# A static scheduler's hand-over estimate goes from 250 to 350, and the first attention's tasks get positions from -32 on

## The chip, the core and the metric

The kernel runs on one core of a Trainium2 chip. TensorE (PE in the profile) multiplies, VectorE (DVE) and ScalarE (ACT) do the elementwise work, GpSimd (POOL) builds the masks once, and SyncE (SP) issues every DMA. The metric is the device time in microseconds (us) of one execution of the whole program; lower is better.

## What is computed

An attention over 4 batches of 8 heads, 576 positions, 64 numbers per head, feeds a network of two layers, all in float32 accuracy:

```python
scores = scale * np.matmul(q, k.transpose(0, 1, 3, 2))
mask_local = (rel >= 0) & (rel < stride)                       # heads 0 to 3, stride 32
mask_strided = (rel >= 0) & (pos % stride == pos.T % stride)   # heads 4 to 7
attn = softmax(np.where(masks, scores, -1e9));  x = attn @ v   # 2304 rows of 512
h = np.maximum(np.maximum(x @ w1, x @ w2), x @ w3)             # 512 -> 768
x = h @ w_out                                                  # 768 -> 512
h = x @ w_in;  g = np.maximum(h, 0) + alpha * np.minimum(h, 0) # 512 -> 2048
out = g @ w_out2                                               # 2048 -> 512
```

## The kernel before

**Arithmetic.** Each float32 operand of the two layers is kept as a pair, a rounded high part and the remainder, and each product is made of three matmuls (high with high, high with low, low with high). The weights arrive as 64-bit numbers. `from_double` turns a block of them into float32 words: a DMA into one of three staging buffers (`raw`), one ScalarE pass (L427, the rebasing) and two VectorE passes (L431 and L433, the word). `split_tasks` then makes the pair: a ScalarE cast (L237) and a VectorE subtraction (L240). Weights of the first layer stay on the chip (18 gate blocks, named by block f and gate g, and 6 output blocks). Weights of the second layer are combined in pairs (`sums`, L500), split, and stored to HBM through two staging tiles (`wst`) for later.

**Attention.** A unit is (batch, head pair cc, half hf). Pairs 2 and 3 are strided heads, 0 and 1 local ones. A unit is a list of tasks: scores on TensorE (L304), per tile a masking that also finds the row minimum (VectorE, L312) and an exponential (ScalarE, L319), a reciprocal (VectorE, L330 and L331), a multiplication by it for each head (`normalise`, on VectorE at L252 or ScalarE at L250), transposes on TensorE (L345), a copy out of PSUM (`keep`, L237, on either engine), the products with v (`values`, L370), and the split of the result into the pair x (a ScalarE cast at L237, a VectorE subtraction at L240).

**First layer.** A gate unit is 12 matmuls (L530) followed by a copy (L616) or a maximum (L619); after the third gate the result is split into h (L625, L240). An output unit is 18 matmuls (L552) and a copy (L599).

**Who sets the order.** Everything up to about 328 us (attention of all four batches, first layer of batches 0 to 2, all weights) is recorded as tasks of a `Weave`. Each task has an engine or two to choose from with an estimated cost in ns, a position `pos`, the things it needs, and the buffers it makes. `Weave.run` plays through the tasks with these estimates and emits them one by one. The engine on which a task could start earliest is served; of its tasks that could start within 120 ns of the first, the one with the lowest position is taken. A task's result counts as there `DELAY` ns after its end. What comes out is a fixed order on every engine; on the chip each engine follows its own order and waits by semaphores. Gate and output units of batch b have positions from 44 b on. Attention units of the first batch have positions spread from `first` to `last` (L719 and L720):

```python
first, last = (-40, -8) if b == 0 else ((b - 1) * NUNITS + (16 if b == 1 else 3), b * NUNITS - 3)
step = (last - first) / (len(ATT_UNITS) + 2)
```

After the weave come the first layer of the last batch and the second layer, written out in a fixed order that this change does not touch. Rings bound what may run ahead: 8 PSUM banks, 2 q and k tiles, 2 v tiles, 3 score tiles, 3 `raw`, 8 words, 2 `wst`.

Of the kernel before, what the change touches and what calls it, by code (L numbers as in the profile page):

```python
# [2 lines left out]

# [35 lines left out]
NUNITS = 2 * (3 * NF1 + NCC)  # L39
# [4 lines left out]
class Weave:  # L44
# [6 lines left out]

    DELAY = {"PE": 300, "ACT": 250, "DVE": 250, "SP": 2300}

    URGENT = 1000

    def __init__(self, rings):
# [4 lines left out]
    def add(self, engines, emit, pos, needs=(), gives=(), makes=(), uses=(), mode=None, slack=0):  # L63
        t = len(self.tasks)
        if engines[0][0] != "PE" and any(key in self.banks for key in uses):
            pos -= self.URGENT
        self.banks.update(key for ring, key in makes if ring == "bank")
        self.tasks.append((engines, emit, pos, needs, makes, mode, slack))
        for ring, key in makes:
            if ring in self.order:  # L70
                self.order[ring].append(key)
        for e in gives:
            self.givers.setdefault(e, []).append(t)
        for key in [key for _, key in makes] + list(uses):
            self.users.setdefault(key, []).append(t)
# [16 lines left out]
                    at = max(at, done[u])  # L92
        return at

    def run(self):
        free = dict.fromkeys(self.DELAY, 0)
        left = [sum(len(self.givers[e]) for e in task[3]) for task in self.tasks]
        takers = {}
        for t, task in enumerate(self.tasks):
            for e in task[3]:  # L100
                for g in self.givers[e]:
                    takers.setdefault(g, []).append(t)
        at = [0] * len(self.tasks)
        ready = {t for t, n in enumerate(left) if not n}
        done, mode = {}, None
        while ready:
            options = {}
            for t in ready:
                engines, _, pos, _, makes, m, slack = self.tasks[t]
                when = self.place(makes, done)  # L110
                if when is None:
                    continue
                when = max(when, at[t] + slack)
                best = None
                for e, cost in engines:
                    start = max(when, free[e])
                    if best is None or start + cost < best[0] + best[2]:
                        best = (start, e, cost)
                start, e, cost = best
                if m is not None:  # L120
                    start += 100 * (m != mode)
                options.setdefault(e, []).append((start, pos - (m is not None and m == mode), t, cost))
            pick = None
            for e, c in options.items():
                first = min(o[0] for o in c)
                o = min((o for o in c if o[0] <= first + 120), key=lambda o: (o[1], o[0], o[2]))
                if pick is None or o[0] < pick[1][0]:
                    pick = (e, o)
            e, (start, _, t, cost) = pick
            _, emit, _, _, makes, m, _ = self.tasks[t]  # L130
            ready.remove(t)
            emit(e)
            for ring, key in makes:
                self.made[ring].append(key)
            mode = mode if m is None else m
            free[e] = start + cost
            done[t] = start + cost + self.DELAY[e]
            for u in takers.get(t, ()):
                left[u] -= 1
                same = e == "PE" == self.tasks[u][0][0][0]  # L140
                at[u] = max(at[u], start + cost if same else done[t])
                if not left[u]:
                    ready.add(u)
        assert len(done) == len(self.tasks)


@with_exitstack
def attention_maxout_prelu_kernel(
# [85 lines left out]
    add, tl = weave.add, {}  # L234
# [34 lines left out]
    def load_task(b, cc, pos):  # L269
        qk, vk = ("q", b, cc), ("v", b, cc)  # L270

        def emit_qk(_):
            q = qkp.tile([P, S], F32, tag="q", name="q")
            nc.sync.dma_start(q, qT[b, cc])
            k = qkp.tile([P, S + 32 * (cc < 2)], F32, tag="k", name="k")
            nc.sync.dma_start(k, kTl[b, cc] if cc < 2 else kTs[b, cc - 2])
            tl[qk] = q, k

        def emit_v(_):
            v = tl[vk] = vp.tile([P, 6 if cc < 2 else 5, 2, D], F32, tag="v", name="v")  # L280
            nc.sync.dma_start(v, vl[b, cc] if cc < 2 else vs[b, cc - 2])

        add(load(592), emit_qk, pos, gives=[qk], makes=[("q", qk)])
        add(load(350), emit_v, pos + 1, gives=[vk], makes=[("v", vk)])

    def attention_tasks(b, cc, hf, pos, step):

        u = (b, cc, hf)
        nq, nk, tiles = geometry(cc, hf)
        n = len(tiles)  # L290
        slack = 1500 if b else 0
        ek, qk, vk = ("e", u), ("q", b, cc), ("v", b, cc)
        banks = [("sc", u, j) for j in range(2)]

        def scores(_):
# [12 lines left out]
            makes=[("bank", key) for key in banks] + [("e", ek)], uses=[qk], mode="scores")  # L308
# [25 lines left out]
        for j in range(2):  # L334
# [13 lines left out]
            def keep(e, trk=trk, ptk=ptk):  # L348
# [3 lines left out]
                gives=[("nrm", u, j)], uses=[ek])  # L352
            add((("PE", 95 * n),), transposes, pos + step, needs=[("nrm", u, j)], gives=[trk],
                makes=[("bank", trk), ("pt", ptk)], uses=[ek], mode="transposes", slack=slack)
# [3 lines left out]
        pvk = ("pv", u)  # L358
        halves = [hf] if cc < 2 else [0, 1]
        xks = [("x", b, cc, h) for h in halves]  # L360
        fresh = [k for k in xks if k not in weave.users]

        def values(_):
# [6 lines left out]
                    nc.tensor.matmul(pv[D * j:D * (j + 1), nq * i:nq * (i + 1)], v[:nk, t, j, :],  # L370
                                     tl["pt", u, j][:nk, nq * i:nq * (i + 1)], start=True, stop=True)

        add((("PE", 2 * n * 85),), values, pos + 2 * step, needs=[vk] + [("pt", u, j) for j in range(2)],
            gives=[pvk], makes=[("bank", pvk)] + [("x", k) for k in fresh],
            uses=[vk] + [("pt", u, j) for j in range(2)] + xks, mode="values", slack=slack)

        def parts(h):
# [8 lines left out]
        for h in halves:  # L386
# [3 lines left out]
                needs=[pvk], gives=[hik], uses=[pvk])  # L390
# [325 lines left out]
    build_constants()  # L716
    nc.sync.dma_start(alpha_sb, alpha)
    for b in range(B):
        first, last = (-40, -8) if b == 0 else ((b - 1) * NUNITS + (16 if b == 1 else 3), b * NUNITS - 3)  # L719
        step = (last - first) / (len(ATT_UNITS) + 2)  # L720
        for i, (cc, hf) in enumerate(ATT_UNITS):
            if i in (0, 2, 4, 5):
                load_task(b, cc, first + step * i - 8)
            attention_tasks(b, cc, hf, first + step * i, step)
# [351 lines left out]
```

## Time and profile before

| | us |
|---|---|
| median of 3 runs (770.6 to 776.38) | 774.55 |
| the profiled execution | 772.29 |
| its span, first to last instruction | 770.2 |
| TensorE matmul busy | 744.1 (97%) |
| TensorE weight loads busy | 723.2 (94%) |
| VectorE busy | 594.6 (77%) |
| ScalarE busy | 457.9 (59%) |

A share is an average over the whole span. How the engines stand in a single stretch is in the rows further down.

### The profile page before, as it was taken

The numbers are of one execution on the slowest core, as the hardware profiler recorded it, in microseconds if no ns is written. First come the engines' busy times: TensorE is split into PE (matmuls) and PEld (weight loads), VectorE is DVE, ScalarE is ACT, GpSimd is POOL, SyncE is SP. The second block draws the span as 40 slices with busy tenths as digits, with TensorE's granted clock in tenths as the row PEclk, the third lists the DMA queues.
The fourth block names the chain that finished last, engine by engine and source line by source line (L and its number), as shares of the span: only waits on it lengthen the run. The fifth ranks groups of instructions, "written<-read, shape, count | busy, mean of one in ns | idle before, by whom it ended". The sixth has DMA issues, their size and how long they took to land.

```text
span 770.2 us, 16100 instructions
## 1 busy us (share of the span) xinstructions
PE 744.1 (97%) x5704; PEld 723.2 (94%) x5704; DVE 594.6 (77%) x1658; ACT 457.9 (59%) x1238; POOL 3.2 (0%) x16
## 2 busy tenths in 40 slices
PE   5899999999989999999999999999999999999997
PEld 4689898999989999999999999999999999999997
DVE  5899998779777796326457988878888877888884
ACT  6997796656768487304246566634656644556561
POOL 1000000000000000000000000000000000000000
PEclk9899999999999999999999999999999999999999
DMA  7467768876879865365947789999888999877361
GB/s 243 157 233 250 222 233 289 297 247 247 291 262 310 274 205 170 120 243 209 342 157 249 264 290 304 381 393 364 286 286 311 347 403 327 271 250 255 119 204 53
DMA packets 85471, 199.37 MB, mean 259 GB/s; under 512 B 10640, under 2 KB 40848, under 8 KB 85392
## 3 DMA queue, kind: packets, MB, share of 16 engines
q1 hardware_dynamic: 85392, 198.35, 74.7%
q8 instruction: 45, 0.74, 0.4%
q14 instruction: 34, 0.28, 0.1%
HBM read 148.51 MB, written 49.81 MB: 258 GB/s over the span
## 4 chain that ended last, share of the span: by engine, by line
PE 60%; DVE 17%; DMA 10%; ACT 8%; issue 3%; SPq 1%; DVEq 0%; ACTq 0%
PE ph L947 20%; PE po L790 15%; PE bank L530 14%; PE bank L552 7%; DMA wh<-w 4%; ACT e L319 2%; DVE word L433 2%; DVE g L784 2%; DMA raw<-in_w 2%; DVE c L794 2%; DVE w L240 2%; PE bank L304 1%; DVE word L431 1%; DVE t L619 1%; PE bank L370 1%
## 5 line engine op out<-in xcount | busy, mean ns | idle before, releaser
L530 PE MATMUL bank<-x,w 128*128 128x288 f32 x1728 | 236.8, 297 | 4.5 <-DVE x L240 1.4
L530 PEld LDWEIGHTS bank<-x,w 128*128 128x128 f32 x1728 | 231.3, 189 | 6.7 <-ACT pt L237 1.7
L947 PE MATMUL ph<-x,w 128*128 128x384 f32 x1008 | 203.3, 337 | 1.1 <-DVE c L952 1.1
L790 PE MATMUL po<-w,g 128*128 128x256 f32 x1296 | 183.8, 282 | 1.7 <-DVE g L784 0.6
L790 PEld LDWEIGHTS po<-w,g 128*128 128x128 f32 x1296 | 175.5, 189 | 4.2 <-DVE g L784 3.2
L947 PEld LDWEIGHTS ph<-x,w 128*128 128x128 f32 x1008 | 168.3, 188 | 2.1 <-DVE c L952 1.8
L952 DVE TENSOR_TENSOR c<-ph,c 128x384 f32<-128x384 f32 x168 | 90.8, 553 | 33.1 <-PE ph L947 32.2
L783 ACT CAST g<-c 128x384 fp32r<-128x384 f32 x96 | 48.5, 505 | 89.7 <-DVE c L934 56.5
L552 PE MATMUL bank<-h,w 128*128 128x288 f32 x576 | 79.5, 297 | 0.4 <-DVE t L619 0.4
L552 PEld LDWEIGHTS bank<-h,w 128*128 128x128 f32 x576 | 76.8, 188 | 1.5 <-DVE t L619 0.6
L240 DVE TENSOR_TENSOR w<-word,w 128x512 fp32r<-128x512 f32 x88 | 55.4, 635 | 26.8 <-ACT w L237 26.5
L319 ACT ACTIVATE e<-e,nm 96x128 f32<-96x128 f32 (+2 forms) x176 | 67.9, 392 | 8.1 <-DVE nm L312 8.0
L904 ACT ACTIVATE c<-c 128x384 f32<-128x384 f32 x96 | 50.4, 525 | 34.0 <-DVE c L952 33.0
L237 ACT CAST w<-word 128x512 fp32r<-128x512 f32 x88 | 50.8, 582 | 31.8 <-DMA wh<-w 15.9
L905 ACT ACTIVATE c<-c,nalpha 128x384 f32<-128x384 f32 x96 | 59.2, 617 | 3.1
L908 DVE SCALAR_TENSOR_TENSOR c<-c 128x384 f32<-128x384 f32 x96 | 52.9, 551 | 8.9 <-ACT c L905 8.9
L784 DVE TENSOR_TENSOR g<-c,g 128x384 fp32r<-128x384 f32 x96 | 52.7, 549 | 1.9 <-ACT g L783 1.9
L784 DVE TENSOR_TENSOR g<-k,g 128x384 fp32r<-128x384 f32 x72 | 36.7, 548 | 14.4 <-ACT g L783 14.4
L427 ACT ACTIVATE word<-raw 128x512 f32<-128x512 f32 x56 | 37.2, 676 | 9.6 <-DMA raw<-in_w 4.8
L433 DVE SCALAR_TENSOR_TENSOR word<-raw,word 128x512 uint32<-128x512 uint32 x56 | 38.8, 692 | 1.9
L619 DVE TENSOR_TENSOR t<-bank,t 128x288 f32<-128x288 f32 x72 | 32.3, 449 | 7.6 <-PE bank L530 4.1
L783 ACT CAST g<-k 128x384 fp32r<-128x384 f32 x72 | 33.4, 516 | 7.8 <-PE po L790 4.4
(72 smaller groups left out, 683.3 us busy)
## 6 DMA issues: line engine op xcount, KB each, us to landing
w<-wh SPq DMA_DIRECT2D x72, 512.0 KB, 4.9
raw<-in_w SPq DMA_DIRECT2D x50, 512.0 KB, 4.6
w<-wo SPq DMA_DIRECT2D x48, 512.0 KB, 5.8
w<-wp SPq DMA_DIRECT2D x36, 512.0 KB, 6.0
wh<-w SPq DMA_DIRECT2D x24, 512.0 KB, 3.5
xd<-xst SPq DMA_DIRECT2D x28, 384.0 KB, 3.3
x<-xd SPq DMA_DIRECT2D x28, 384.0 KB, 8.1
wp<-w SPq DMA_DIRECT2D x24, 256.0 KB, 3.2
```

The lines of the kernel that those rows point to most:

```text
L240: nc.vector.tensor_tensor(out=out_, in0=x, in1=y, op=ALU.subtract)
L319: nc.scalar.activation(tl[ek][:nq, j, i, :nk], tl[ek][:nq, j, i, :nk], AF.Exp, bias=tl["nm", u][:nq, j, i:i + 1], scale=-1.0, accum_out=tl ...
L433: nc.vector.scalar_tensor_tensor(out=a, in0=raw[:, :, 0], scalar=29, in1=a, op0=ALU.logical_shift_right, op1=ALU.bitwise_or)
L530: nc.tensor.matmul(acc, words["gate", f, g][:, wi, cc * P:(cc + 1) * P], xt[b, cc, hf][:, xi, :], start=n == 0, stop=n == 3 * NCC - 1)
L552: nc.tensor.matmul(acc, words["mix", f][:, wi, dc * P:(dc + 1) * P], st["h", hf, f][:, xi, :], start=n == 0, stop=n == 3 * NF1 - 1)
L783: nc.scalar.copy(g[:, 0], x)
L784: return g, lambda: nc.vector.tensor_tensor(out=g[:, 1], in0=x, in1=g[:, 0].bitcast(F32), op=ALU.subtract)
L790: nc.tensor.matmul(bank[:, NH * half:NH * (half + 1)], g[:, gi, t * P:(t + 1) * P], w[:, wi, off:off + NH], start=first and i == 0, stop=l ...
L905: nc.scalar.activation(a, a, AF.Copy, scale=nalpha[:, f:f + 1])
L908: nc.vector.scalar_tensor_tensor(out=a, in0=h, scalar=0.0, in1=a, op0=ALU.max, op1=ALU.add)
L947: nc.tensor.matmul(bank, words["h", n, i][:, wi, off + c * P:off + (c + 1) * P], x2h[blk, k, c][:, xi, :], start=m == 0, stop=m == 5)
L952: nc.vector.tensor_tensor(out=out_, in0=bank, in1=other, op=ALU.add)
```

## The change

Two numbers of the plan change. A task that ends on ScalarE or VectorE now counts as handed over 350 ns after its end, not 250. The first batch's attention units get positions from -32 to -8, not from -40 to -8, so that the step between two units is 2.4 and not 3.2. `run` is divided into `plan`, which makes the order, and the loop that emits it. The other settings of `plan` have the values that stood there before (120, 100, 1.0, no random shift). For strided units, the second half's `values` now needs the first half's to have been placed (`begun`), as the first half makes the x tile that both fill.

```diff
-    DELAY = {"PE": 300, "ACT": 250, "DVE": 250, "SP": 2300}
-
     URGENT = 1000
@@
-    def run(self):
-        free = dict.fromkeys(self.DELAY, 0)
+    def plan(self, seed=None, near=120, change=100, slack=1.0, delay=350, shift=0.0):
+
+        rng = random.Random(seed)
+        sway = [rng.uniform(-shift, shift) if task[2] > -self.URGENT / 2 else 0.0 for task in self.tasks]
+        delays = {"PE": 300, "ACT": delay, "DVE": delay, "SP": 2300}
+        self.made = {ring: [] for ring in self.rings}
+        free = dict.fromkeys(delays, 0)
@@
-                when = max(when, at[t] + slack)
+                when = max(when, at[t] + slack * wait)
@@
-                o = min((o for o in c if o[0] <= first + 120), key=lambda o: (o[1], o[0], o[2]))
+                o = min((o for o in c if o[0] <= first + near), key=lambda o: (o[1], o[0], o[2]))
@@
-            done[t] = start + cost + self.DELAY[e]
+            done[t] = start + cost + delays[e]
@@
+    def run(self, **settings):
...
+        for t, e in self.plan(**settings):
+            self.tasks[t][1](e)
@@
-        add((("PE", 2 * n * 85),), values, pos + 2 * step, needs=[vk] + [("pt", u, j) for j in range(2)],
-            gives=[pvk], makes=[("bank", pvk)] + [("x", k) for k in fresh],
+        begun = ("x begun", b, cc)
+        add((("PE", 2 * n * 85),), values, pos + 2 * step,
+            needs=[vk] + [("pt", u, j) for j in range(2)] + ([begun] if cc >= 2 and hf else []),
+            gives=[pvk] + ([begun] if cc >= 2 and not hf else []), makes=[("bank", pvk)] + [("x", k) for k in fresh],
@@
-        first, last = (-40, -8) if b == 0 else ((b - 1) * NUNITS + (16 if b == 1 else 3), b * NUNITS - 3)
+        first, last = (-32, -8) if b == 0 else ((b - 1) * NUNITS + (16 if b == 1 else 3), b * NUNITS - 3)
```

The change moves instructions on all engines throughout the weave. In the changed kernel a line number of the weave's tasks is 10 to 12 higher (L240 is L250, L431 is L443). Three places follow.

VectorE in the first batch's attention, before: the first gate weight's word (L431, L433) stands between the reciprocal of the last strided unit and its multiplication.

```order
L252 TENSOR_SCALAR e<-e,rc 108x108 x3
L330 TENSOR_SCALAR rc<-sm 126x2x2
L331 RECIPROCAL rc<-rc 126x2x2
L431 TENSOR_SCALAR word<-word 128x512
L433 SCALAR_TENSOR_TENSOR word<-raw,word 128x512
L252 TENSOR_SCALAR e<-e,rc 126x126 x2
```

VectorE, changed: the same word (now L443, L445) stands 33 rows further down, behind the masking of two more local units.

```order
L322 ISA e,nm<-bank,mask_l 96x128
L322 ISA nm 96x1
L262 TENSOR_SCALAR e<-e,rc 96x128 x3
L340 TENSOR_SCALAR rc<-sm 96x6
L341 RECIPROCAL rc<-rc 96x6
L443 TENSOR_SCALAR word<-word 128x512
L445 SCALAR_TENSOR_TENSOR word<-raw,word 128x512
L262 TENSOR_SCALAR e<-e,rc 96x128 x6
```

The word moved behind attention work; in the old place the multiplications of the strided unit (x4) follow the reciprocal at once.

TensorE where the first layer of batch 2 begins (216 us in the trace), before: a gate unit of batch 2 (L530 x12) stands ahead of batch 1's output units (L552).

```order
L304 MATMUL bank<-k,q 108x108 x6
L370 MATMUL bank<-pt,v 64x96 x12
L345 MATMUL bank<-ident,e 128x96 x12
L530 MATMUL bank<-x,w 128x288 x12
L370 MATMUL bank<-pt,v 64x96 x12
L552 MATMUL bank<-h,w 128x288 x54
L530 MATMUL bank<-x,w 128x288 x24
```

The same place, changed.

```order
L314 MATMUL bank<-k,q 108x108 x6
L380 MATMUL bank<-pt,v 64x96 x12
L355 MATMUL bank<-ident,e 128x96 x12
L564 MATMUL bank<-h,w 128x288 x18
L380 MATMUL bank<-pt,v 64x96 x12
L564 MATMUL bank<-h,w 128x288 x54
L542 MATMUL bank<-x,w 128x288 x96
```

All four output units now come before the first gate unit of batch 2.

ScalarE at the same place, before: two casts of second-layer weights and two rebasings stand ahead of the casts of x and the four copies of transposes.

```order
L616 COPY t<-bank 128x288
L237 CAST w<-word 128x512 x2
L427 ACTIVATE word<-raw 128x512 x2
L625 CAST h<-t 128x288
L237 CAST x<-bank 128x288 x2
L237 COPY pt<-bank 128x288 x4
```

The same place, changed.

```order
L247 CAST w<-word 128x256
L637 CAST h<-t 128x288
L247 CAST x<-bank 128x288
L329 ACTIVATE e,sm<-e,nm 108x108 x2
L247 CAST x<-bank 128x288
L247 COPY pt<-bank 128x288 x3
L247 CAST w<-word 128x512 x2
```

The two casts moved behind x and the copies, of which the fourth went to VectorE.

## Rows read from the trace of the kernel before

**Rows 1.** Busy time by stretch: window, its length, busy us of each engine, clock, DMA.

```profile
0.00:44.20 44.20, 31.73 (x278) 24.95 (x278) 31.56 (x195) 35.95 (x149) 3.22 (x16) 0.92 0.61 201
44.20:125.20 81.00, 78.36 (x654) 74.58 (x655) 76.75 (x232) 66.19 (x199) 0.00 (x0) 1.00 0.74 246
125.20:225.20 100.00, 96.48 (x810) 92.88 (x812) 80.65 (x285) 66.11 (x218) 0.00 (x0) 0.98 0.78 268
...
328.00:770.20 442.20, 434.68 (x3081) 430.75 (x3080) 336.17 (x712) 224.90 (x467) 0.00 (x0) 1.00 0.78 274
```

**Rows 2.** TensorE in order of time: start, us, what, and the idle time before.

```profile
27.27 0.72 PE L345 MATMUL bank<-ident,e 96*128 96x96 f32 x3 [1.59 <-DVE e L252]
...
35.59 1.84 PE L530 MATMUL bank<-x,w 128*128 128x288 f32 x12
...
43.14 0.53 PE L530 MATMUL bank<-x,w 128*128 128x288 f32 x2
44.48 15.78 PE L530 MATMUL bank<-x,w 128*128 128x288 f32 x117 [0.81 <-DVE w L240]
```

**Rows 3.** Busy time from VectorE's first instruction to the third weight's remainder.

```profile
6.79:44.43 37.64, 30.20 (x266) 23.39 (x264) 31.79 (x196) 34.90 (x149) 0.00 (x0) 0.91 0.60 202
```

**Rows 4.** VectorE in order of time.

```profile
20.25 0.39 DVE L431 TENSOR_SCALAR word<-word 128x512 uint32<-128x512 uint32 x1
20.67 0.69 DVE L433 SCALAR_TENSOR_TENSOR word<-raw,word 128x512 uint32<-128x512 uint32 x1
...
27.85 0.68 DVE L252 TENSOR_SCALAR e<-e,rc 96x128 f32<-96x128 f32 x3
28.44 0.45 DVE L237 COPY pt<-bank 128x288 f32<-128x288 f32 x1
...
37.32 0.17 DVE L330 TENSOR_SCALAR rc<-sm 96x6 f32<-96x6 f32 x1 [1.02 <-ACT e L319]
...
42.61 0.26 DVE L312 CUSTOM_DVE_ANT_0 e<-bank,mask_s 108x108 f32<-108x108 f32 x1
...
43.74 0.69 DVE L240 TENSOR_TENSOR w<-word,w 128x512 fp32r<-128x512 f32 x1
...
57.76 0.69 DVE L240 TENSOR_TENSOR w<-word,w 128x512 fp32r<-128x512 f32 x1
```

**Rows 5.** ScalarE in order of time.

```profile
34.47 0.99 ACT L250 ACTIVATE e<-e,rc 96x128 f32<-96x128 f32 x3
35.36 0.38 ACT L237 COPY pt<-bank 128x288 f32<-128x288 f32 x1
35.63 0.41 ACT L319 ACTIVATE e<-e,nm 96x128 f32<-96x128 f32 x1
...
37.19 0.61 ACT L237 CAST w<-word 128x512 fp32r<-128x512 f32 x1
...
38.84 1.24 ACT L427 ACTIVATE word<-raw 128x512 f32<-128x512 f32 x2
```

**Rows 6.** Busy time and granted clock (the column after POOL) around the two slow-clock stretches.

```profile
24.00:28.00 4.00, 1.98 (x15) 1.11 (x11) 3.70 (x23) 4.00 (x21) 0.00 (x0) 0.87 0.74 250
28.00:32.00 4.00, 4.00 (x32) 3.27 (x34) 3.86 (x23) 3.68 (x16) 0.00 (x0) 0.50 0.36 106
...
222.00:225.00 3.00, 2.95 (x12) 2.90 (x12) 2.97 (x14) 3.00 (x13) 0.00 (x0) 0.51 0.98 298
```

**Rows 7.** TensorE's later waits in the weave, in order of time.

```profile
125.20 1.88 PE L530 MATMUL bank<-x,w 128*128 128x288 f32 x12 [1.36 <-DVE x L240]
...
220.50 0.47 PE L345 MATMUL bank<-ident,e 96*128 96x96 f32 x3 [1.45 <-DVE t L619]
222.05 3.13 PE L530 MATMUL bank<-x,w 128*128 128x288 f32 x12 [1.08 <-ACT pt L237]
```

**Rows 8.** VectorE at a second-layer weight, in order of time.

```profile
213.65 0.69 DVE L240 TENSOR_TENSOR w<-word,w 128x512 fp32r<-128x512 f32 x1 [2.41 <-ACT w L237]
```

**Rows 9.** The chain of waits, in order of time: start, us, what.

```profile
57.91 4.64 DMA raw<-in_w
```

More of the change, by code (lines that the diff above doesn't have):

```diff
@@ L1 @@
 import math
+import random
 from contextlib import ExitStack
@@ L93, in place @@
         return at
-    def run(self):
-        free = dict.fromkeys(self.DELAY, 0)
-        left = [sum(len(self.givers[e]) for e in task[3]) for task in self.tasks]
[L98 to L102, printed above, removed]
+    def plan(self, seed=None, near=120, change=100, slack=1.0, delay=350, shift=0.0):
[4 more added lines that the diff above has]
+        free = dict.fromkeys(delays, 0)
+        left = [sum(len(self.givers[e]) for e in task[3]) for task in self.tasks]
         at = [0] * len(self.tasks)
         ready = {t for t, n in enumerate(left) if not n}
-        done, mode = {}, None
+        done, mode, order = {}, None, []
         while ready:
@@ L108, in run @@
             for t in ready:
-                engines, _, pos, _, makes, m, slack = self.tasks[t]
+                engines, _, pos, _, makes, m, wait = self.tasks[t]
                 when = self.place(makes, done)
@@ L120, in run @@
                 if m is not None:
-                    start += 100 * (m != mode)
-                options.setdefault(e, []).append((start, pos - (m is not None and m == mode), t, cost))
+                    start += change * (m != mode)
+                options.setdefault(e, []).append(
+                    (start, pos + sway[t] - (m is not None and m == mode), t, cost))
             pick = None
@@ L129, in run @@
             e, (start, _, t, cost) = pick
-            _, emit, _, _, makes, m, _ = self.tasks[t]
+            makes, m = self.tasks[t][4:6]
             ready.remove(t)
-            emit(e)
+            order.append((t, e))
             for ring, key in makes:
@@ L136, in run @@
             free[e] = start + cost
-            done[t] = start + cost + self.DELAY[e]
-            for u in takers.get(t, ()):
+            done[t] = start + cost + delays[e]
+            for u in self.takers.get(t, ()):
                 left[u] -= 1
@@ L144, in run @@
         assert len(done) == len(self.tasks)
+        return order
+    def run(self, **settings):
+        self.takers = {}
+        for t, task in enumerate(self.tasks):
+            for e in task[3]:
+                for g in self.givers[e]:
+                    self.takers.setdefault(g, []).append(t)
+        for t, e in self.plan(**settings):
+            self.tasks[t][1](e)
 @with_exitstack
```

## The prediction

> **What bounds the kernel now.** I read the busy time by stretch first. From 44.2 us on TensorE works almost without a gap: 78.4 of 81.0 us, then 96.5 of 100 us, and 434.7 of 442.2 us in the part that the change leaves alone. Only the first 44.2 us are different: TensorE 31.7, VectorE 31.6, ScalarE 36.0 [rows 1]. The work of TensorE is the same before and after, so a new order is worth what TensorE waits less, or runs less at a low clock, before 328 us. The rows give the stock. Idle TensorE time is 12.5 us up to 44.2, 2.6 up to 125.2, 3.5 up to 225.2 [rows 1]. To this comes the clock: 0.50 of 28 to 32 us and 0.51 of 222 to 225 us, that is its 1.2 GHz level [rows 6]. Twelve gate matmuls took 3.13 us there and 1.88 us at 125.2, so the second low stretch cost 1.25 us [rows 7].
>
> The order of time shows who is late. In the first attention TensorE waits for multiplications by VectorE (1.59 us) and at 44.48 for the remainder of the third gate weight (0.81 us); two of that unit's twelve matmuls ran at 43.14, so in effect the unit began at 44.2 [rows 2]. Later waits are the x of batch 1 (1.36 us at 125.20), a maximum (1.45 us) and copies of transposes (1.08 us) at 220 to 222 [rows 7].
>
> **The count itself.** The trace shows a hand-over directly: VectorE's remainder ends at 43.74 + 0.69 = 44.43 and TensorE's matmul starts at 44.48 [rows 2, 4]. That is 0.05 us; both 250 and 350 ns are longer. The change therefore doesn't make the plan truer to one hand-over; it only puts other work between maker and user. What follows goes by the order alone. The split into plan and emission, and the settings that keep their values, move nothing. The added need orders two `values` groups of equal work and adds no instruction; it costs nothing, since the other group stands ready on TensorE.
>
> **First stretch, up to the third weight.** TensorE has the same tasks ahead of the first product on the third gate weight in both orders, so only the time of that weight counts. Ahead of it on VectorE, five copies (0.45 each), one multiplication (0.59, from 27.85 to 28.44) and a maximum (0.45) leave, 3.3 us; three multiplications (one of them two thirds as long, 1.6) and three copies (1.35) come, 2.9 us [rows 4]. On ScalarE, three multiplications (0.89, 0.89, 0.6), three copies (0.27), a rebasing (0.6) and two exponential steps (1.56 from 35.63 to 37.19) leave, 5.3 us; one multiplication and five copies come, 2.2 us [rows 5]. In that time VectorE is idle for 37.64 - 31.79 = 5.85 us and ScalarE for 2.7 us [rows 3]. ScalarE, the fuller one, loses 3.1 us of work; the gain is at most VectorE's idle time, 5.85 us and the 0.4.
>
> How much of that is got I worked out by following the tasks. Up to 17 us both orders go at the pace of TensorE's unchanged first tasks. The first gate weight's word, made from 20.25 to 21.36 before [rows 4], now comes after the maskings of two more units, so its remainder arrives last of all that the first product needs. That costs two steps more on VectorE ahead of the product (0.59 and 0.69); against it, ScalarE reaches the x of the second local unit 0.8 us of work earlier and VectorE 0.3 us. I take the first product at the old time, 35.6 [rows 2], between 34.7 (0.9 us earlier, if TensorE keeps its clock in the scores and values ahead of it) and 36.9 (both added steps in full).
>
> From there VectorE's queue is known, and no wait shows in it: a copy 0.45, a reciprocal 0.51 (37.32 to 37.83 in the row's own place), a word 1.1 (0.42 from 20.25 to 20.67, and 0.69), a multiplication 0.59, the third weight's word 1.1, the second weight's remainder 0.69, x 0.45, five pairs of maskings at 0.38 (three take 1.13 from 42.61 to 43.74), the third remainder 0.69. The sum is 7.5 us, against 8.84 now (35.59 to 44.43), of which 1.02 is a wait for an exponential [rows 2, 4]. So the third weight is there at 43.1, not 44.43, and TensorE starts on it 1.1 us sooner than the 44.2. **A = -1.1 us**, bounds -5.9 and +0.2 (the product at 36.9).
>
> **Up to 125 us.** VectorE is the pace here: busy 76.75 of 81.0 us [rows 1], and it hands over the x for which TensorE waits 1.36 us [rows 7]. Ahead of that x, three remainders of second-layer weights (0.69 each at most) and four subtractions of `sums` (0.45 each, an estimate from the copy of a like width) leave VectorE, two pairs of maskings come (0.8), and seven multiplications and five copies take the place of four and six (+1.3 by the durations above). One of those remainders is of half width. That makes about 1.3 us less in all. On TensorE the scores of one unit of batch 2 (0.8 us) now stand ahead of the same product. TensorE comes 1.1 us earlier with 0.8 us more to do, VectorE 1.1 + 1.3 us earlier: the wait closes. **B = -1.4 us**, bounds -2.6 (all idle time of this stretch) and +1.2 (A given back, if VectorE only keeps its old time).
>
> **At 216 to 225 us.** The output units now cover the wait for x: 18 matmuls stand between the transposes and the values, 54 behind. Two casts and two rebasings are out of ScalarE's way. But VectorE stood idle for 2.41 us just before, for a cast that waited for a store's buffer [rows 8], and the maximum that frees TensorE's bank is behind such a remainder in both orders. If the stores keep their time, VectorE has from 213.65 on, in the new order, a remainder 0.69, an h 0.45, a half remainder 0.45, a maximum 0.45, four subtractions 1.8, a maximum 0.45, three pairs of maskings 1.13 and the last h 0.45. That is 5.9 us of durations that overlap by some 0.1 us each, so it ends near 219. TensorE, now 2.5 us ahead, waits there about as long as it does now and may fall to 1.2 GHz again. It then starts at 219 where it started at 222.05: 3.05 us earlier, so C adds 0.55. If the stores move up with everything else, both waits (2.53) and the 1.25 of clock go: 3.8. I take **C = -0.7**, near the lower end, because the row shows a wait for a store and not for TensorE; bounds -3.8 and +2.6 (all that was won is waited for here).
>
> **Sum.** 1.1 + 1.4 + 0.7 = 3.2 us. The profiled execution becomes 772.29 - 3.2 = 769.1. It lies 2.3 us under the median of the runs shown; on that scale 774.55 - 3.2 = **771.4 us**, 0.4% faster. One per cent (7.7 us) is about what a measurement of this kernel can tell from no change, so this counts as no change.
>
> **Rivals.** *The gain is waited away.* The stores of the second layer's weights begin some 6 us of VectorE work later in the new order, and the stretch up to 225 us ends when they do. Then TensorE is ahead at 125 us and back at its old time at 225 us: 774.5 us. For it speaks the 2.41 us; against it, that the casts at the place itself stand no later in ScalarE's order.
>
> *The clock.* Before each low stretch TensorE was busy for half of the time or less: 1.98 of 4.0 us from 24 to 28 [rows 6], and 2.53 us idle in two waits at 220 to 222 [rows 7]. If the new order closes those gaps, TensorE stays at 2.4 GHz: A is 0.9 us better, C is the full 3.8, and the sum is 2.0 + 1.4 + 3.8 = 7.2 us: 767.4 us. Against it: the multiplication that starts the second transposes of the first local unit comes only 0.6 us earlier by the count above, so 1 of the 1.59 us gap stays. The Trainium skill, "TensorE: Matmul & The Clock Gate", section "What's actually happening", says that the throttled state is the default and activity releases it; by that rule a first attention with fewer gaps would be spared the low stretch as well. The trace's two low stretches, each behind idle time, agree.
>
> *Slower: the weights come late.* The first weight's word moves from 21 to about 28 us, as it now stands behind the multiplication that starts TensorE's transposes at 27.27 [rows 2]; the second's moves back too. There are three staging buffers, so the fourth and fifth fetches start that much later. A fetch takes 4.64 us to land [rows 9]. The place is 45 to 70 us; the ninth weight's remainder ends at 58.45 [rows 4] and TensorE takes it up at 44.2 + 9 x 1.6 = 58.6, a margin of 0.15 us. By my count the margin becomes 1 us, as the third word comes earlier. It decides from the point where the fourth word is more than 1 us behind it: TensorE then waits one landing for each of two weights, 9.3 us, less the 1.1 won and the 3.9 of later waits that this fills (1.36, 1.45 and 1.08): +4.3, 778.9 us.
>
> *Not doing what it says* would be an order that hardly changes; it is excluded, as the order of all engines differs.
>
> **How the numbers follow.** Forecast (1 to 6 us faster) 0.55; gain waited away 0.2; clock 0.13; slower 0.12. The range takes the first two whole, half of the clock's and some of the slower one's: 767.0 to 777.0. Faster by over 1% (under 766.8) needs the clock's case and a little more: 0.08. Slower by over 1% (above 782.3) needs late weights twice over: 0.04. The rest is 0.88.
>
> **What would show it.** Right: the first gate matmuls start at 34.7 to 36.9 us, the long run of them by 43 us, the wait for x near 122 us is gone, and the part behind the weave lasts 442 us as before. Wrong: a wait of gate matmuls for VectorE's remainders (w) between 45 and 70 us; a wait for a copy behind a cast that waits for a store near 135 us; new low-clock stretches. I would be wrong by more than the range if VectorE stood idle in the first 44 us for longer than now.

## The result and the profile after

The changed kernel takes 765.94 us (median of 6 runs, 764.72 to 767.51) beside 774.51 us for the kernel before on the same chip: a ratio of 0.990, 95% interval 0.988 to 0.993. Twice more beside other runs it came to 0.993 (0.990 to 0.995) and 0.991 (0.989 to 0.993). Over 98 runs on the later chips the kernel before had medians of 772.0 to 773.2 us, so the gain is 6.4 to 8.6 us. 3.2 were forecast, and the time lies 1.1 us under the range.

The profiled execution took 764.85 us (span 762.9). TensorE in order of time, after (start, us, what, idle time before):

```profile
14.16 1.10 PE L355 MATMUL bank<-ident,e 126*126 126x126 f32 x4
...
26.47 0.72 PE L355 MATMUL bank<-ident,e 96*128 96x96 f32 x3 [2.22 <-DVE e L262]
...
35.53 3.23 PE L542 MATMUL bank<-x,w 128*128 128x288 f32 x12
...
42.35 17.86 PE L542 MATMUL bank<-x,w 128*128 128x288 f32 x133
...
117.89 0.82 PE L314 MATMUL bank<-k,q 64*108 64x108 f32 x12
...
121.48 1.00 PE L314 MATMUL bank<-k,q 64*126 64x126 f32 x8 [0.49 <-ACT pt L247]
...
211.08 0.82 PE L314 MATMUL bank<-k,q 64*108 64x108 f32 x12
...
214.62 2.64 PE L564 MATMUL bank<-h,w 128*128 128x288 f32 x18 [0.44 <-DVE nm L322]
...
318.20 19.20 PE L542 MATMUL bank<-x,w 128*128 128x288 f32 x144
```

These answer to [rows 2, 7]. The first gate product starts where it was forecast (35.53; 35.59 before), but its twelve matmuls take 3.23 us and not 1.84. The wait for x of batch 1, the two waits at 220 to 222 us and the slow product there are gone; 0.49 us of waiting for a copy and 0.44 for VectorE are left at these places. Busy time and granted clock (the column after POOL) around those places, after; they answer to [rows 6]:

```profile
24.00:28.00 4.00, 1.78 (x14) 1.44 (x14) 3.93 (x24) 4.00 (x21) 0.00 (x0) 0.78 0.74 246
28.00:32.00 4.00, 4.00 (x37) 3.27 (x34) 3.44 (x23) 3.05 (x11) 0.00 (x0) 0.50 0.71 223
32.00:36.00 4.00, 3.21 (x26) 2.50 (x23) 3.34 (x20) 3.43 (x15) 0.00 (x0) 0.50 0.14 56
36.00:40.00 4.00, 4.00 (x26) 3.50 (x26) 3.51 (x11) 3.04 (x12) 0.00 (x0) 0.51 0.39 108
...
44.00:60.00 16.00, 16.00 (x123) 16.00 (x122) 15.51 (x34) 13.43 (x41) 0.00 (x0) 1.00 0.81 253
...
216.00:225.00 9.00, 9.00 (x84) 8.72 (x83) 6.81 (x18) 7.29 (x24) 0.00 (x0) 1.00 0.70 229
```

The clock fell at the end of the 2.22 us wait and stayed at its 1.2 GHz level until almost 40 us, twice as long as before. At 216 to 225 us it is 1.00. From 44 to 60 us TensorE is busy for all 16 us, and the run of gate matmuls there takes 0.134 us for each (17.86 for 133), as in the last batch (19.20 for 144), so no weight came late.

To see where the gain arises, idle time isn't enough; the start of the same matmul in both traces is. Five rows of the kernel before that serve for this, TensorE:

```profile
86.95 1.29 PE L345 MATMUL bank<-ident,e 126*126 126x126 f32 x4 [0.65 <-ACT e L250]
...
120.74 0.82 PE L304 MATMUL bank<-k,q 64*108 64x108 f32 x12
...
159.97 0.59 PE L345 MATMUL bank<-ident,e 126*126 126x126 f32 x4
...
216.20 0.82 PE L304 MATMUL bank<-k,q 64*108 64x108 f32 x12
...
325.84 19.20 PE L530 MATMUL bank<-x,w 128*128 128x288 f32 x144
```

The same tasks of TensorE lie ahead of each of these places in both orders. The third gate weight is taken up at 43.96 (42.35 and twelve matmuls of 0.134), before at 44.2. The scores of batch 2's next unit start at 117.89 and not 120.74, those of batch 3 at 211.08 and not 216.20, the last batch's gate units at 318.20 and not 325.84. So 0.25 us are won up to 44 us, 2.6 more up to 120, 2.3 more up to 216, 2.5 more up to 326, and 0.3 are lost behind the weave. One row also shows why idle time says too little: the four transposes at 86.95 took 1.29 us, at 159.97 0.59. 0.7 us of waiting stands inside the first group and counts as busy.

### The profile page after: what moved, and what is told of

It reads as the page before. It is cut to its first block, busy times and chain, and to the rows that moved or that the text cites. A ratio compares the mean times of both kernels' runs of the same rounds, so it can differ in the third digit from the quotient of the medians.

```text
span 762.9 us, 16093 instructions
## 1 busy us (share of the span) xinstructions
PE 741.8 (97%) x5704; PEld 723.0 (95%) x5704; DVE 596.8 (78%) x1670; ACT 454.7 (60%) x1226; POOL 3.2 (0%) x16
## 4 chain that ended last, share of the span: by engine, by line
PE 77%; DVE 12%; DMA 5%; ACT 2%; issue 2%; SPq 1%; DVEq 0%; ACTq 0%
PE bank L542 27%; PE ph L959 20%; PE po L802 15%; PE bank L564 9%; PE bank L314 3%; PE bank L380 2%; PE bank L355 2%; DVE g L796 2%; DVE c L806 2%; DMA w<-wh 1%; DMA w<-wp 1%; DVE e L322 1%; DMA xs<-x 1%; DMA x<-xd 1%; DVE c L964 1%
## 5 line engine op out<-in xcount | busy, mean ns | idle before, releaser
L250 DVE TENSOR_TENSOR w<-word,w 128x512 fp32r<-128x512 f32 x88 | 55.4, 637 | 23.9 <-ACT w L247 23.5
L445 DVE SCALAR_TENSOR_TENSOR word<-raw,word 128x512 uint32<-128x512 uint32 x56 | 38.8, 693 | 1.9
```

The source lines that it names most:

```text
L250: nc.vector.tensor_tensor(out=out_, in0=x, in1=y, op=ALU.subtract)
```

## Experiments

The edits are shown against the changed kernel, and against the kernel before where its filled gaps are the subject. A ratio with its 95% interval is that of the whole comparison; it can differ by 0.1 to 0.2% from the quotient of two medians.

Three theories were tried at first. **H**: a longer hand-over makes an order with fewer waits. **F**: the later positions of the first attention do it. **P**: every setting draws another order of the same list, as good as its luck, and the planner's own estimates already tell how good. The end of the plan, that is the planned start of its last task when `plan` plays the list through, is 321.1 us for the kernel before (321.5 with the need `begun`, the number the expectations use) and 313.4 for the changed one. Later the question was the slow clock of the first attention (theory **K**).

**Delay alone, positions alone.**

```diff
-        first, last = (-32, -8) if b == 0 else ...
+        first, last = (-40, -8) if b == 0 else ...
```

> Hand-over 350 as in the changed kernel, positions from -40 as before. Theory H (a longer hand-over makes a sturdier order): nearly all of the gain of 8.6 us comes, 766 to 767.5 us. Theory F (the positions of the first attention make the gain): as before, 773 to 775. Theory P (every setting draws another order of the same list, and the end that the plan itself works out with its own estimates tells which is shorter): the plan ends at 315.4 us here, against 321.5 before and 313.4 changed, so 768 to 769.5.

Measured: 768.34 us, 0.995 of before (0.993 to 0.997). About half of the gain: P's range is met, H's is missed.

```diff
-    def plan(self, seed=None, near=120, change=100, slack=1.0, delay=350, shift=0.0):
+    def plan(self, seed=None, near=120, change=100, slack=1.0, delay=250, shift=0.0):
```

> Positions from -32 as in the changed kernel, hand-over 250 as before. Theory H: no gain, 773 to 776 us. Theory F: most of the gain, 766 to 768. Theory P: the plan ends at 318.2, so 770.5 to 772.5.

Measured: 772.51 us, 1.000 (0.997 to 1.003). F is out. Its 12 executions lie between 767.43 us (mean granted clock 0.995) and 778.89 (0.982), and the time goes with the clock: the five at 0.991 or more took 767.43 to 771.76 us, the seven below that 772.40 to 778.89.

**Other lengths of the hand-over**, positions from -32.

```diff
-delay=350
+delay=200
```

> Positions from -32, and the hand-over made shorter than before, 200. Theory H: slower than before, 775 to 779 us, since more waits for ScalarE and VectorE open up. Theory F: 766 to 768. Theory P: the plan ends at 314.0, as early as in the changed kernel to 0.6 us, so 766 to 768; if this comes, the length of the hand-over isn't the cause.

Measured: 768.26 us, 0.995 (0.992 to 0.998). A hand-over shorter than before's gains too: H is out, and P's 766 to 768 is met but for 0.3 us. Two later runs put P to a harder test, since they lie on the wrong sides for H.

```diff
-delay=350
+delay=340
```

> The changed kernel with a hand-over of 340 in place of 350. Theory H (the length counts): as the changed kernel, 0.990 to 0.993 of before. Theory P (another draw, told by the plan's own end): the plan ends at 322.3 us, 0.8 later than before's, so 1.000 to 1.004 of before, 772 to 775 us.

Measured: 771.00 us, 0.997 (0.995 to 0.999). Ten nanoseconds less, and some two thirds of the gain are gone. P had the direction, but forecast 1.000 to 1.004.

```diff
-delay=350
+delay=220
```

> The changed kernel with a hand-over of 220, shorter than before's 250. Theory H: slower than before. Theory P: the plan ends at 311.1, 2.3 us ahead of the changed kernel's, so 0.987 to 0.991 of before, 762 to 765 us.

Measured: 764.71 us, 0.989 (0.987 to 0.992), as P has it.

**One order early, the other late.** The planner's clock decides which hand-over a task counts.

```diff
-            done[t] = start + cost + delays[e]
+            hand = 250 if start < 45000 else 350
+            done[t] = start + cost + (hand if e in ("ACT", "DVE") else delays[e])
```

with positions from -40:

> Before's order to 45 us of the plan (positions from -40, 250), 350 for what ends later. Theory H: all that was gained behind 44 us, 7.1 of 7.3 us, so 766 to 768 us. Theory F: 774. Theory P: the plan ends at 312.2, earlier than the changed kernel's, so 764 to 766. The clock's low stretch is short again here (6.8 us, as before) if the order of the first attention sets it.

Measured: 766.42 us, 0.993 (0.991 to 0.995). The first attention as before, and still most of the gain. P's 764 to 766 is missed by 0.4 us and H's 766 to 768 is met, so this run doesn't speak against H; hand-overs of 200 and 220 do. The low stretch of the clock isn't the forecast 6.8 us but about 3.3 (0.59 from 28 to 32 us, 0.99 behind), with before's order in the first attention: the order alone doesn't set it.

The reverse, with positions from -32:

```diff
+            hand = 350 if start < 45000 else 250
```

> The changed kernel's order up to 45 us of the plan (positions from -32, 350), 250 behind it. If the longer hand-over is needed where the gain arises, behind 44 us: 772 to 775, as the kernel before, less the 0.3 us won up to there. If only another order is needed, and the end that the plan works out for itself tells its worth: the plan ends at 314.4, so 767 to 769.

Measured: 769.41 us, 0.997 (0.994 to 0.999). Just outside P's forecast of 767 to 769, and nearer to it than to the 772 to 775 of its rival.

Before's order still longer, positions from -40:

```diff
+            hand = 250 if start < 190000 else 350
```

One difference to before's order lies ahead of that point: near 177 us of the plan `begun` turns two groups of `values` round, and some tasks around them move. By itself `begun` was not tried; alone it moves the plan's end by 0.4 us.

> Before's order up to 190 us of the plan (positions from -40, 250), 350 behind it: TensorE's order first differs where batch 1's output units go ahead of the first gate unit of batch 2, the place of term C. Prediction's value of C: 0.7 us faster than before, with a wait of TensorE near 219 us. If C is as large as the two traces have it: 2.5 to 3.5 us faster, and no wait over 0.5 us and no slow clock at 216 to 225 us. If the stores set the time there: as before, within 0.5 us.

Measured: 773.10 us, 1.001 (0.999 to 1.004): nothing is won. Yet at the place itself the trace has what was hoped for. TensorE, this run:

```profile
127.64 3.25 PE L543 MATMUL bank<-x,w 128*128 128x288 f32 x12 [2.44 <-DVE x L251]
...
220.19 0.82 PE L315 MATMUL bank<-k,q 64*108 64x108 f32 x12
...
223.09 2.68 PE L565 MATMUL bank<-h,w 128*128 128x288 f32 x18
...
326.79 19.20 PE L543 MATMUL bank<-x,w 128*128 128x288 f32 x144
347.77 27.50 PE L543 MATMUL bank<-x,w 128*128 128x288 f32 x194 [1.78 <-DVE t L554]
```

From 220.19 to 326.79 are 106.6 us, against 109.6 before. But in this execution the wait for x was longer and its product slow (3.25 us), and behind the weave TensorE waited 1.78 us for a maximum (before: 0.97). A gain that a trace shows at one place isn't yet a gain of the total.

**The slow clock.** Into the gaps of the first attention go matmuls without use: transposes of the identity into the bank of the next real transposes, which overwrite it. Nothing of the computation is left out.

```diff
             def transposes(_, j=j, trk=trk, ptk=ptk):
                 tr = tl[trk] = bank()
...
+                for _ in range({(0, 2, 0, 0): 14, (0, 3, 0, 1): 10, (0, 0, 0, 1): 16, (0, 0, 1, 0): 5}.get((*u, j), 0)):
+                    nc.tensor.transpose(tr[:126, :126], ident[:126, :126], ident[:126, :126])
                 for i in range(n):
```

> The changed kernel, with idle matmuls put into TensorE's four largest gaps of the first attention (14, 10, 16 and 5 transposes of 126 x 126 of the identity, ahead of the real ones, in the same bank, which overwrite it). Theory K (the slow clock of the first attention follows from those gaps, and it ate what A promised): the clock stays at 1.0, TensorE begins the first gate product at 33 to 35 us and the third weight by 42.5, and the time is 2 to 4 us under the changed kernel's, 761 to 764 us. Rival (VectorE and ScalarE set the pace there, and the slow clock only fills time in which TensorE would wait): the clock rises, the waits for multiplications grow by as much, and the time stays within 1 us of the changed kernel's.

Measured: 764.27 us, 0.991 (0.988 to 0.994), on another chip than the first comparison. K's signs in the trace came (clock 1.00, the first gate product at 32.91 us and not 35.53), but its 761 to 764 us is missed by 0.3, and with a ratio of 0.990 to 0.993 for the changed kernel this run alone doesn't show that filling wins anything there. The same kernel again, beside the changed one and the filled kernel before on one chip:

> The changed kernel beside the filled ones, on one chip: 0.990 to 0.993 of before.

> The kernel before with filled gaps (14, 8 and 11): 0.994 of before again. This is what the slow clock of the first attention cost the kernel before.

> The changed kernel with filled gaps. If the slow clock costs both orders the same: as much under the changed kernel as the filled kernel before is under before, 0.985 to 0.987 of before. If before loses more to it, and part of the gain is the clock: 0.989 to 0.992, that is the order alone worth 2 to 4 us, and not the 6 to 8 seen without filling.

Measured, with 772.66 us for before: changed 765.21 (0.991), before filled 767.02 (0.993, 0.991 to 0.996), changed filled 763.20 (0.989, 0.986 to 0.992). The second of three expectations for the filled changed kernel came. In us:

| | gaps as they are | gaps filled | filling |
|---|---|---|---|
| before's order | 772.66 | 767.02 | -5.6 |
| changed order | 765.21 | 763.20 | -2.0 |
| order | -7.5 | -3.8 | |

Filling the first attention of the kernel before had already been tried:

```diff
+                for _ in range({(0, 2, 0, 0): 14, (0, 3, 0, 1): 8, (0, 0, 0, 1): 11}.get((*u, j), 0)):
+                    nc.tensor.transpose(tr[:126, :126], ident[:126, :126], ident[:126, :126])
```

> The kernel before, with the same idle matmuls in three gaps of the first attention (14, 8 and 11). With the clock kept up there, what is left of the difference to the changed kernel with its gaps filled is the order alone. Theory K: 1.5 to 3 us faster than before; the slow stretch at 222 us stays. If the slow clock only fills waiting time: as before, within 0.5 us.

Measured: 767.57 us, 0.994 (0.992 to 0.996), more than theory K's upper end of 3 us. With all runs together, filling is worth 0.6% in before's order and 0.1% in the changed one: 4 us of difference, with an uncertainty of about 3. So about half of the gain is there with filled gaps too, and the other half is that filling does more for the kernel before. The two fillings aren't alike (14, 8 and 11 idle transposes against 14, 10, 16 and 5).

That doesn't mean that the changed order is spared the slow clock. The mean granted clock is 0.9929 over 98 executions of the kernel before and 0.9936 over 18 of the changed one. As 1.2 GHz is half of 2.4, that is about 11 and 10 us of an execution at the low level. With filled gaps it is 0.9982 (19 executions) and 0.9986 (10), about 3 and 2 us. Filling takes some 8 us of slow clock off both orders. These 8 us cost the kernel before 5 us and the changed one 1 to 2; why they cost it less isn't shown.

The changed kernel with the gaps filled, TensorE:

```profile
9.22 3.20 PE L355 MATMUL bank<-ident 126*126 126x126 f32 x14
...
14.34 0.65 PE L357 MATMUL bank<-ident,e 126*126 126x126 f32 x4
...
23.44 1.88 PE L355 MATMUL bank<-ident 126*126 126x126 f32 x16
25.74 0.69 PE L357 MATMUL bank<-ident,e 96*128 96x96 f32 x3 [0.41 <-DVE e L262]
...
38.24 6.99 PE L544 MATMUL bank<-x,w 128*128 128x288 f32 x48
```

and its windows, in the columns of [rows 6]:

```profile
24.00:28.00 4.00, 3.59 (x41) 2.89 (x40) 3.93 (x25) 4.00 (x22) 0.00 (x0) 1.00 0.65 230
28.00:32.00 4.00, 3.23 (x36) 2.45 (x36) 3.96 (x32) 4.00 (x17) 0.00 (x0) 1.00 0.83 277
```

The clock keeps its 2.4 GHz level, and the long run of gate matmuls starts at 38.24, 4.1 us earlier than the 42.35 of the changed kernel's first profile. Half of that reaches the end (the span is 760.9 us); the rest is lost on the way, in part to a wait of 1.1 us for a maximum by VectorE.

The same matmuls in the kernel before with filled gaps: two executions of one and the same kernel. TensorE, first the run beside the changed kernel (765.22 us):

```profile
123.36 1.89 PE L532 MATMUL bank<-x,w 128*128 128x288 f32 x12 [2.00 <-DVE x L240]
...
212.72 0.82 PE L304 MATMUL bank<-k,q 64*108 64x108 f32 x12
...
216.43 1.88 PE L532 MATMUL bank<-x,w 128*128 128x288 f32 x12 [0.61 <-ACT pt L237]
...
319.64 30.58 PE L532 MATMUL bank<-x,w 128*128 128x288 f32 x227
```

then the earlier one (771.62 us):

```profile
215.64 0.82 PE L304 MATMUL bank<-k,q 64*108 64x108 f32 x12
...
219.17 0.47 PE L347 MATMUL bank<-ident,e 96*128 96x96 f32 x3 [0.68 <-DVE t L621]
220.72 2.62 PE L532 MATMUL bank<-x,w 128*128 128x288 f32 x12 [1.09 <-ACT pt L237]
...
325.85 4.38 PE L532 MATMUL bank<-x,w 128*128 128x288 f32 x32
```

From the scores to the last batch's gate units it is 106.9 us in one and 110.2 in the other. So the loss at 216 to 225 us is not a fixed property of the order; in the second execution the clock is 0.51 from 222 to 225 us, in the first 1.00. What differs ahead of it is ScalarE's cast that waits for a store's buffer. ScalarE, in the same two runs:

```profile
206.93 0.62 ACT L237 CAST w<-word 128x512 fp32r<-128x512 f32 x1 [0.45 <-DMA wh<-w]
```

```profile
211.60 0.62 ACT L237 CAST w<-word 128x512 fp32r<-128x512 f32 x1 [1.87 <-DMA wh<-w]
```

and in the trace of the kernel before that the prediction rests on:

```profile
212.99 0.62 ACT L237 CAST w<-word 128x512 fp32r<-128x512 f32 x1 [2.72 <-DMA wh<-w]
```

The cast starts 5.8, 4.0 and 3.2 us ahead of the scores, and the stretch behind them takes 106.9, 110.2 and 109.6 us: the early cast goes with the short stretch. That the late store is the cause is argued from these three, not tried.

**The other filled kernels.** The version that draws early as before (positions from -40) and late with 350, filled with 14, 8 and 11:

```diff
+            hand = 250 if start < 45000 else 350
...
+                for _ in range({(0, 2, 0, 0): 14, (0, 3, 0, 1): 8, (0, 0, 0, 1): 11}.get((*u, j), 0)):
```

> Before's order to 45 us of the plan, 350 behind it, and idle matmuls in three gaps of the first attention (14, 8 and 11). By theory K 1 to 3 us under the same kernel without them, 763.5 to 765.5, since one slow stretch of 3.4 us is left there to win. By the rival the same as without them, 766.4.

Measured: 764.41 us, 0.992 (0.989 to 0.995). The time lies in K's range; beside 0.993 for the same kernel unfilled, the gain can't be told from none.

C alone (350 from 190 us of the plan on, positions from -40), filled:

```diff
+            hand = 250 if start < 190000 else 350
...
+                for _ in range({(0, 2, 0, 0): 14, (0, 3, 0, 1): 8, (0, 0, 0, 1): 11}.get((*u, j), 0)):
```

> Before's order up to 190 us of the plan, 350 behind it, gaps filled. If the gain of C that the trace of the unfilled version has (3 us at 216 to 225 us) stays in the total, 2 to 3.5 us under the filled kernel before. If the part behind the weave gives it back (a later landing of the rows that VectorE subtracts there), within 1 us of it.

Measured: 766.09 us, 0.993 (0.990 to 0.996), beside 767.57 for the filled kernel before: 1.5 us, between the two forecasts, with intervals that overlap. C is small; whether it is 0 or 1.5 us stays open.

One gap of the changed kernel alone:

```diff
+                for _ in range({(0, 0, 0, 1): 16}.get((*u, j), 0)):
```

> The changed kernel with idle matmuls in its largest gap alone (16, ahead of the 2.2 us wait at 26.5 us, behind which the slow stretch began). If that gap alone sets the stretch off: the clock 1.0 from there on, 764 to 765 us. If the earlier gaps count too: a slow stretch is left, and the time is between this and the changed kernel's.

Measured: 765.21 us, 0.991 (0.989 to 0.994); the clock is 1.00 from 24 to 36 us in the profiled execution, but 0.57 from 36 to 40. So a slow stretch is left, as the second expectation has it, but the changed kernel lies too close on this chip to tell the times apart:

> The changed kernel once more, beside the others on one chip: 0.990 of the time before, and single executions that differ with the time spent at the slow clock, at about 0.5 us for each us of it.

Measured: 766.47 us, 0.993 (0.990 to 0.995), where 0.990 was expected. The rule of 0.5 us for each us at the slow clock doesn't show in these six runs (764.71 and 768.54 both have a mean granted clock of 0.993).

The version that the runs pointed to, hand-over 220 with its gaps filled:

```diff
-delay=350
+delay=220
...
+                for _ in range({(0, 2, 0, 0): 14, (0, 0, 0, 0): 28, (0, 1, 1, 0): 4}.get((*u, j), 0)):
```

> Hand-over 220 with its three gaps of the first attention filled (14, 28 and 4). Theory P with the clock kept up: 1 to 2 us under the same order without filling, 0.986 to 0.989 of before, 762 to 764 us, and the fastest version here.

Measured: 765.06 us, 0.990 (0.987 to 0.992): no better than the same order unfilled (0.989), and not the fastest. The fastest median is the changed kernel with filled gaps, 763.20 us; against the changed kernel beside it this is 2.0 us, within the uncertainty of both.

**The plan's end and the time**, orders without filled gaps (the changed kernel as the mean of its three comparisons):

| order | plan's end, us | ratio to before |
|---|---|---|
| 220, from -32 | 311.1 | 0.989 |
| 250 then 350, from -40 | 312.2 | 0.993 |
| changed: 350, from -32 | 313.4 | 0.991 |
| 200, from -32 | 314.0 | 0.995 |
| 350 then 250, from -32 | 314.4 | 0.997 |
| 350, from -40 | 315.4 | 0.995 |
| 250, 350 from 190 us, from -40 | 317.6 | 1.001 |
| 250, from -32 | 318.2 | 1.000 |
| before: 250, from -40 | 321.1 | 1 |
| 340, from -32 | 322.3 | 0.997 |

The three orders with the earliest end are the three fastest. The lengths of the hand-over, where there is one alone, stand in no order: 220, 350, 200, 350, 250, 250, 340. Among the last four the plan's end no longer tells which is faster.

## Why the prediction was wrong

**The failing step is B**, the stretch from the third gate weight to the wait for x: -1.4 us, with all idle time of the stretch (2.6) as its bound, and nothing forecast from there to 216 us. The mechanism was right, the size wrong. The wait for x did close: five traces with before's order have it at 1.16 to 2.44 us, six with the changed order not at all (0.49 to 0.59 us for a copy instead). But this wait lies behind the scores at 120.74. The first two traces have 4.9 us: 2.6 up to those scores, and 2.3 from there to 216, of which the wait for x is 1.36. The mean over more executions is 3.8. For this I took six traces with the changed order and, with before's, five up to the scores of batch 2 and three from there to those of batch 3, filled and unfilled ones, since the stretches begin behind the gaps, at the end of the third weight's remainder: 76.6 against 74.4 us, and 95.4 against 93.8.

Two mistakes made B small. Idle time isn't a bound, since waits inside a group of matmuls count as busy: up to 120 us TensorE shows 1.28 us of idle time before and none after, and still 2.6 us were won (0.7 more stood inside the group at 86.95). VectorE's own lead was counted as 2.4 us, but TensorE's visible idle time was taken as what it could bring. The x for which TensorE had waited was ready 3.65 us earlier. VectorE, before and after:

```profile
124.69 0.45 DVE L240 TENSOR_TENSOR x<-bank,x 128x288 fp32r<-128x288 f32 x1
```

```profile
121.04 0.45 DVE L250 TENSOR_TENSOR x<-bank,x 128x288 fp32r<-128x288 f32 x1
```

And the waits between 126 and 216 us were left out of the sum, though [rows 1] has 3.5 us of idle time from 125.2 to 225.2, of which C used 2.5.

**A** (-1.1) was about right. The first product came at 35.53, as forecast. In the first profile, with its longer slow clock, the third weight's remainder ended at 43.91, 0.5 us ahead of before's 44.43. VectorE, after:

```profile
43.22 0.69 DVE L250 TENSOR_TENSOR w<-word,w 128x512 fp32r<-128x512 f32 x1
```

In two later ones of the changed kernel it ended at 43.03 and 42.28. The mean, 43.1, is the forecast, and 1.6 us earlier than the 44.6 of three executions with before's first attention (44.43, 45.45, 44.02). With such a spread, that the mean meets the forecast to 0.1 us is luck in part.

**C** (-0.7) measured 2.5 us in the first two traces, 1.6 in the mean (108.9 in three executions of before's order, 107.3 in six of the changed one, and the two overlap: 106.9 to 110.2 and 106.4 to 108.5). Tried by itself it gave 0 unfilled and 1.5 filled. That is nearer to the forecast than the traces are. The reason given for the low value was wrong: the stores don't keep their time. In the changed kernel the cast and VectorE's remainder moved up by 4.4 and 4.0 us, with everything else. ScalarE and VectorE, after; the second answers to [rows 8]:

```profile
208.59 0.62 ACT L247 CAST w<-word 128x512 fp32r<-128x512 f32 x1 [1.24 <-DMA wh<-w]
```

```profile
209.69 0.68 DVE L250 TENSOR_TENSOR w<-word,w 128x512 fp32r<-128x512 f32 x1
```

**Not forecast**: the part behind the weave is 0.3 us longer in the first two traces (1 us in the mean of the same three and six), where "as before" was forecast.

**The rivals.** The gain was not waited away by the stores. Late weights are excluded by the full pace of the gate matmuls from 44 to 60 us, and TensorE has no wait at all from 126 to 160 us. The clock rival came nearest in time (767.4), but not by what it said: the stretch at 222 us vanished, the one in the first attention grew, and over many executions the changed kernel has about as much slow clock as the kernel before (0.9936 and 0.9929). That filled gaps take 5 us off the kernel before and 1 to 2 off the changed one shows that a part of the gain, about 4 us of it with an uncertainty of 3, is that the changed order loses less by the same slow time; how this divides between the slow matmuls themselves and later waits for stores stays open. The Trainium skill, "TensorE: Matmul & The Clock Gate", section "What's actually happening", has the throttled state as the default that activity releases. By that rule the filled gaps keep the clock up, and the traces agree (1.00 from 24 to 32 us, where it was 0.78 and 0.50).

**The count itself** was rightly read: a longer hand-over doesn't make the plan truer. Orders with 200 and 220 gain as well, and 340 loses most of it. But having said that the order alone counts, I followed some tens of tasks by hand at three places. The planner's own sum over the whole list, 7.7 us shorter, was there to be read, and lies within what was measured. That it meets the size is luck in part: it gives 10.0 us for 220, where 8.4 were measured, and a loss for 340, which gained.

## What to carry to other kernels

Where a greedy planner sets the order, its settings are draws, not knobs: try many, rank them by the planner's own end, and run the best few; a neighbouring value may lose most of it. Count what an order can win by when the same instruction starts, not by idle time, and over several executions, as one trace's waits for stores and slow stretches come and go with the same order. Before reordering, fill the gaps ahead of the first long run of matmuls: here that alone gave the kernel before 5 us, though the changed one only 1 to 2 and the order of 220 nothing that could be measured.

## What the hardware showed that was not expected

Executions of one kernel differ by more than the change is worth: with the positions alone, from 767.43 to 778.89 us, at mean granted clocks from 0.996 to 0.982. There the time goes with the clock; over the 98 executions of the kernel before it does so only weakly (correlation 0.39).

The granted clock reads 1.00 where TensorE is slow. From 12 to 16 us of the changed kernel, whose row follows, four transposes of 126 x 126 take 1.10 us; four like them take 0.65 us at 21.09.

```profile
12.00:16.00 4.00, 4.00 (x28) 3.15 (x29) 3.37 (x23) 2.87 (x13) 0.00 (x0) 1.00 0.85 292
```

With 14 idle transposes ahead they take 0.65 us already at 14.34.

The idle matmuls were transposes alone. With them, and with nothing else changed, the granted clock is 1.00 from 24 to 32 us, where it was 0.78 and 0.50.
